# Gated mix of two attentions: three shared PSUM banks, raises in place, query tiles through DRAM, adding DMAs, and 372 blocks on VectorE

## The chip, the cores and the metric

The kernel runs on one core of a Trainium2 chip. The metric is the device time of one execution in microseconds (us); the time before is the median of three runs.

## The reference, cut to what matters

Two attentions over the same input are mixed by a gate of each row. S = 2048 rows, D = 512 columns, H = 32 heads of Dh = 16; everything is bfloat16.

```python
x = A_x
g = sigmoid((x * gate_w).sum(-1, keepdims=True))
# A: full attention, every row against every row
qkv = split(x @ A_wqkv)                                # q, k, v: H heads of 16
p = softmax(einsum("bhqd,bhkd->bhqk", q, k) * Dh ** -0.5)
a = einsum("bhqk,bhkd->bhqd", p, v) -> rows @ A_wo
# B: eight rows behind each row, two apart (row, row-2, ... row-14)
idx = pos[:, None] - 2 * arange(8)[None, :]; mask = idx >= 0
logits = einsum("bhsd,bhswd->bhsw", q, k[idx]) * Dh ** -0.5, -1e9 where masked
b = einsum("bhsw,bhswd->bhsd", softmax(logits), v[idx]) -> rows @ B_wo
out = g * a + (1 - g) * b
```

## The kernel before

**Attention A.** The 2048 queries are cut into four chunks of 512, and the heads into eight groups of four. A chunk and a group make a *period*; there are 32, in order of chunks. In a period the scores are computed transposed, in *blocks* of 128 keys by 512 queries: 16 key tiles by 4 heads, 64 blocks a period and 2048 in all. A head uses a strip of 32 rows of TensorE's array (16 for the keys, 16 for a bound that keeps the exponential in range, for which the queries' other 16 rows hold absolute values), so that blocks of different heads can run side by side. The key rows of all heads lie in `kt_all`, the values with a column of ones in `vp_all`.

**Two ways through the exponential.** Most blocks go to ScalarE: three or two blocks make a *set* (`qk`, into the PSUM rings rA and rB of three and two banks), one instruction takes the exponential of the set (`ex`, pT<-ring), and TensorE multiplies the result with the values into the sums of the period (`pv_run`, PSUM bank `acc`). The others go to VectorE (`d_set`, numbers a period in `n_dve`, 339 in all, always from the last three key tiles). A single score product fills the PSUM bank `D`; VectorE turns it into a 16-bit integer by one multiplication and addition (`p1`, dt_a<-D or wkv<-D: the second half of the buffers is the memory of the key and value weights, from period 8 on), which read as a bfloat16 is a rough power of two. Four *variants* of it, the integer raised by 0, 32, 64 and 96, are each multiplied with values that carry a weight of their own (`vd_all`, `NV` = 4), and their sum smooths the error. Three blocks make a group (`NGR`), so that one raise serves three blocks (`sh`, pd_a<-dt_a or pd_a<-wkv). Before, three raises of a group read the converted integers and write into one of three buffers `pd_a` each. Source and target are cut differently, six runs of 256 values into three runs of 512.

**End of a period.** `po1` transposes the sums out of PSUM (accT<-acc), the denominators are inverted (`po2`) and multiplied in (GpSimd, ott<-accT), `po3` transposes back, and after eight periods the output projection of the chunk follows (`ab_part`, `ab_ev`), which also adds in attention B.

**Queries.** `q_proj` makes the query tile of a period: 16 products of 32 columns from a copy of the weights in which each head's columns stand twice (`wq2`), a cast (qt<-misc_ps) and a mask that removes signs from half of the rows (qt<-qt,qmask).

**Attention B.** `b_tile` works on 128 rows at a time, 16 tiles. Keys and values are projected, written to DRAM (kv_scr) by SP's queue and gathered back shifted, four shifts at a time (ksh, vsh, three buffers `gat`). The arithmetic is GpSimd's, mostly on 256 columns an instruction: products with the queries (prod<-ksh,qb), additions that halve the row (prod<-prod, lg<-prod), a softmax together with VectorE and ScalarE (lg, mx, rr), products of values and weights (prod<-vsh,lg) and their additions (`av_add`: prod<-prod, ob<-ob,prod, ob<-prod, obb<-ob,prod; 14 a tile). At the end TensorE transposes obb into `obt`.

**Order of the work.** Nothing is issued as it comes: every step is an `Op` with an engine, a cost, a due time, predecessors and tokens of the buffers that it takes (`tok`, `Res`). `list_schedule` lays them out with a model of the chip, and the program is written in that order; `chain_on` fixes it on each engine. The model knows that some VectorE instructions and GpSimd's instructions exclude each other (`SB`, `GP`, the variable `port`). Idle time of TensorE is filled with products of zeros (`zeros`). All engines run in order, so an instruction that waits holds up everything behind it on its engine; this goes for SP's queue of DMAs too.

**PSUM.** Eight banks: five for the rings, one `acc`, one `D`, one `misc` for everything else (`misc_ps`).

Of the kernel before, what the change touches and what calls it, by code (L numbers as in the profile page):

```python
# [19 lines left out]
    n_dve=(3, 3, 6, 6, 6, 9, 9, 9) + (12,) * 24,  # L20
    dve_tiles=3,
# [15 lines left out]
DEXP = 56  # L37
NV = 4
NGR = 3
NPD = 3  # L40
# [5 lines left out]
NDL = 4  # L46
SPREAD = (0.75, 0.8)
STEP = 32.0
WEIGHTS = (0.240234375, 0.2021484375, 0.169921875, 0.142578125)
# [10 lines left out]

class Tok:
    def __init__(self, res):
        self.res, self.ops = res, []


class Op:

    def __init__(self, eng, occ, fn, dl, deps=(), alloc=(), use=(), lat=None, rel=0.0, name="",
                 mode="f", js=(), full=0.0, fill=False, scores=None, after=(), ride=False, parts=None):
        self.scores, self.ride, self.parts = scores, ride, parts  # L70
# [17 lines left out]
GFIRST = -300.0  # L88
PRE = 0.14
GP = lambda kind, n: [(False, PRE), (True, NS[kind] * n)]  # L90
# [11 lines left out]
P1D, SHD, LASTD, PO1D = -100.0, 2.0, 200.0, 300.0  # L102
# [56 lines left out]
def list_schedule(ops, zeros):  # L159
# [15 lines left out]

    def avail(o):
        t = o.ready
        for tk in o.alloc:
            r = tk.res
            n = len(r.order)  # L180
            if n >= r.cap:
                for u in r.order[n - r.cap].ops:
                    if u.done is None:
                        return INF
                    t = max(t, u.end + SELF[u.eng] if u.eng == o.eng else u.done)
        return t

    arr = Array()

    def start(e, o):  # L190
        t = avail(o)
        if t == INF:
            return t, 0.0
        if e != "pe":
            return max(free[e], t), o.dl
        t0, end, _, _ = arr.plan(o, t)
        rides = o.mode == "r" and arr.mode == "r" and end < arr.end + 0.05
        return t0, o.dl + ((ALONE if o.ride else KEEP) if o.mode != arr.mode else 0.0) - (RIDE if rides else 0.0)
# [3 lines left out]
    while len(out) < len(ops):  # L202
# [24 lines left out]
        if e == "pe":  # L227
            tz, n = arr.idle(o, t)
            if n > 0:
                z = zeros(n)  # L230
                tz = max([tz, avail(z)] + [u.t for tk in z.alloc[0].res.order[-2:] for u in tk.ops if u.done is not None and u.t < t])
                if tz + n * PASS + (0.0 if o.mode == "c" else SWITCH) <= t + 0.05:
                    for tk in z.alloc:
                        tk.res.order.append(tk)
# [3 lines left out]
        for tk in o.alloc:  # L238
            tk.res.order.append(tk)
# [16 lines left out]
        out.append(o)  # L256
        for s_ in succ.get(o, ()):
            left[s_] -= 1
            if left[s_] == 0:
                s_.ready = max([s_.rel] + [d.end + SELF[d.eng] if d.eng == s_.eng else d.done for d in s_.deps] + [d.t for d in s_.after])  # L260
                cand[s_.eng].append(s_)
# [4 lines left out]
def kernel(  # L266
# [29 lines left out]

    def misc_ps(shape, dtype=FP32, tag="misc"):
        return ps.tile(shape, dtype, tag=tag, bufs=1, name="misc_ps")
# [50 lines left out]
    def op(eng, occ, fn, dl, **kw):  # L349
        if any(tk.res is res.get("misc") for tk in kw.get("use", ())):  # L350
            dl -= URG[eng]
# [65 lines left out]
    wq2 = const.tile([128, DC, H, 2, DH], BF16, name="wq2")  # L417
# [6 lines left out]
    NH = NG // 2  # L424
    woarr = const.tile([128, NH, D], BF16, name="woarr")
    ident = const.tile([128, 128], BF16, name="ident")
    identf = const.tile([128, 128], FP32, name="identf")
    rowc = const.tile([128, 3], FP32, name="rowc")
    wts = const.tile([128, NV], BF16, name="wts")
# [7 lines left out]
    vd_all = const.tile([128, NV, NTD, H, DH + 1], BF16, name="vd_all")  # L437
# [4 lines left out]
    dt_a = const.tile([128, NDE * NGR * QW], BF16, name="dt_a")  # L442
    pd_a = const.tile([128, NPD * NGR * ROW], BF16, name="pd_a")
    wkv_l = wkv[:].rearrange("p c n -> p (c n)")
    dt_bufs = [dt_a[:, k_ * NGR * QW:(k_ + 1) * NGR * QW] for k_ in range(NDE)]
    dt_bufs += [wkv_l[:, k_ * NGR * QW:(k_ + 1) * NGR * QW] for k_ in range(NDL - NDE)]
    pd_bufs = [pd_a[:, k_ * NGR * ROW:(k_ + 1) * NGR * ROW].rearrange("p (q n) -> p q n", q=NGR) for k_ in range(NPD)]
    stage = [pd_a[:, k_ * DC * D:(k_ + 1) * DC * D].rearrange("p (c n) -> p c n", c=DC) for k_ in range(2)]
    ott2 = const.tile([128, 2, BPC, 32], BF16, name="ott2")
# [3 lines left out]
    e1 = const.tile([128, NT], FP32, name="e1")  # L453
    d1 = const.tile([128, NT], FP32, name="d1")

    def init_dve():
# [9 lines left out]
        for m in range(NV):  # L466
            V.memset(wts[:, m:m + 1], WEIGHTS[m] * 2.0 ** -DEXP)

# [10 lines left out]
    def init_pool2():  # L479
        make_identity(nc, identf[:])  # L480
# [19 lines left out]
    def load_x(sc):  # L500
        def s():
            xl = work.tile([128, W // 2, D], BF16, name="xld", tag="gat", bufs=NGA) if sc < NGA else stage[1]
# [4 lines left out]
    wst = {}  # L507

    def load_w(part):
        def s():  # L510
            if part == 0:
                wst["q"] = stage[0]
                out = wst["q"]
            else:
                out = wkv[:, :, (part - 1) * D:part * D]
# [17 lines left out]

    tw = tok("pd", NPD)
    xtok = [tok("gat", NGA) if sc < NGA else tok("pd", NPD) for sc in range(NC)]
# [6 lines left out]
    o_wq = op("sp", 0.5, load_w(0), -8.5, lat=12.5, alloc=[tw])  # L542
# [13 lines left out]
    def q2(E, i):  # L556
        def s():
            a0 = wst["q"][:, :, 4 * i * DH:4 * (i + 1) * DH]
# [6 lines left out]
    o_q2 = [op("dve", 0.5, q2(V, 0), 0.0, deps=[o_wq], use=[tw])]  # L565
    o_q2 += [op("pool", 1.5, q2(G, i), 4.0 + i, deps=[o_wq, o_k3[1]], use=[tw]) for i in range(1, NG)]
# [5 lines left out]
    o_warm = op("pe", 4.0, warm, -9.0, deps=[o_init_d], alloc=[tok("misc", 1)])  # L572
# [34 lines left out]
    def k_proj(i, sc, tag, dl, rel=0.0):  # L607
        st = {}
        tk = tok(tag, 1)
# [16 lines left out]
    def k_bound(i, dl):  # L626
        st = {}
        tk = tok("acc" if i == 0 else "misc", 1)
# [28 lines left out]
    for i in range(NG):  # L657
        o_kc[i] = []
        for sc in range(NC):
            if i == 0:  # L660
                o_kc[i].append(k_proj(i, sc, ("misc", "acc", "D", "misc")[sc], -2.0 + sc))
# [7 lines left out]
    def v_proj(h0, h1, tb, TB, tag, dl, rel=0.0):  # L669
        n = (h1 - h0) * DH  # L670
        st = {}
        tk = tok(tag, 1)
# [18 lines left out]
        def evd():  # L691
# [3 lines left out]
                            in0=_ap(vp_all[:, t0, h0, 0:1], [list(vp_all[:].ap[0]), [0, NV], [H * (DH + 1), nt], [1, n_]]),  # L695
                            in1=_ap(w, [list(w.ap[0]), [1, NV], [0, nt], [0, n_]]), op=ALU.mult)
# [7 lines left out]
        if nt > 0:  # L704
            d = op("dve", 0.0, evd, dl + 2.0, deps=[c], parts=TT(NV * nt * (h1 - h0) * (DH + 1)))
# [15 lines left out]
    def q_proj(pi, tag, dl, rel=0.0):  # L721
        c_, i = periods[pi]
        st = {}
        tk = tok(tag, 1)
        tq = tok("qt", 3)
        q_tok[pi] = tq

        def part(c0, c1):
            def s():
                if c0 == 0:  # L730
                    st["p1"] = misc_ps([128, QW], tag=tag)
                    qt_tiles[pi] = work.tile([128, QW], BF16, name="qt", tag="qt", bufs=3)
# [17 lines left out]
    for pi in range(1, NP):  # L750
        q_proj(pi, "misc", S0[pi] - 10.0, rel=S0[pi - 1] - 6.0 if pi > 1 else Q1REL)
# [3 lines left out]
    tzp, tzr = tok("misc", 1), tok("misc", 1)  # L755
# [10 lines left out]
    def zsig():  # L766
        A.activation(out=e1[:], in_=st_g["zp"][:, 0:NT], func=ACT.Exp, scale=-1.0)

    def zgate():
        V.tensor_scalar_add(out=d1[:], in0=e1[:], scalar1=1.0)  # L770
        V.reciprocal(out=g_sp[:], in_=d1[:])
        V.tensor_tensor(out=omg[:], in0=e1[:], in1=g_sp[:], op=ALU.mult)

    def zrows():
        st_g["zr"] = misc_ps([128, NT, TPC])
        for s_ in range(TPC):
            for j in range(4):
                mm(st_g["zr"][32 * j:32 * j + 32, :, s_], identf[:, 32 * s_:32 * s_ + 32], g_sp[:], True, True,
# [16 lines left out]
    WH = W // 2  # L795
# [3 lines left out]
    def b_tile(t):  # L799
# [26 lines left out]
        tk = tok("misc", 1)  # L826
# [3 lines left out]
        tk = tok("misc", 1)  # L830
# [539 lines left out]
```

## Time and profile before

| | us |
|---|---|
| median of 3 runs (825.62 to 826.81) | 826.49 |
| the profiled execution, its own time | 826.04 |
| its span, first to last instruction | 824.3 |
| ScalarE busy | 785.9 |
| TensorE busy (ends modelled) | 777.9 |
| GpSimd busy | 720.4 |
| VectorE busy | 706.3 |

The page names engines PE (TensorE), PEld (its weight loads), DVE (VectorE), ACT (ScalarE), POOL (GpSimd) and SP (the queue that issues DMAs). A group's row gives line, engine, operation, what is written and read, shapes and count; then busy time in us, the mean of one in ns, the idle time ahead of its instructions, and what ended most of it. As many instructions are recorded by a helper, most have the same line (L323, L332) and are told apart by the names of their tiles. Neighbouring instructions of an engine overlap by some hundredths of a microsecond, so busy time is less than count times mean. Issuing a DMA isn't counted as busy.

### The profile page before, as it was taken

To read this page: it belongs to the slowest core of one execution; us is meant where nothing else is said; L and a number is where in the kernel's file an instruction comes from. 1 tells how busy PE (TensorE), PEld (TensorE's weight loads), DVE (VectorE), ACT (ScalarE), POOL (GpSimd) and SP (SyncE) were. 2 spreads that over 40 slices of the span, in tenths; PEclk is the share of its full clock that TensorE was granted. 3 is DMA by queue.
4 is the path that set the end of the run, shared out by engine and by line. 5 is a ranking of instruction groups with operands and counts; after the bars stand their busy time and mean duration, and the time that the engine had idled before them with its cause. 6 is when DMAs were issued, how large, how long until landed. Compare 5 with 4: busy or idle time off the path is not lost.

```text
span 824.3 us, 18657 instructions
## 1 busy us (share of the span) xinstructions
PE 777.9 (94%) x7314; PEld 247.4 (30%) x7358; DVE 706.3 (86%) x1111; ACT 785.9 (95%) x706; POOL 720.4 (87%) x1196
## 2 busy tenths in 40 slices
PE   7999999999999999999999999999999999999996
PEld 4333433333322222222222222222222222222231
DVE  5456876788978999989999899999989899998987
ACT  3899999999899899999999999999999999999995
POOL 5097999999999999899999999899999999899960
PEclk9899999999999999999999999999999999999999
DMA  9203020112111220211112111211111211110000
GB/s 296 78 3 116 2 90 28 65 52 65 57 48 65 65 66 28 63 53 47 63 35 77 57 50 51 65 53 49 43 52 54 82 34 65 52 52 27 27 1 26
DMA packets 44440, 47.37 MB, mean 57 GB/s; under 512 B 2352, under 2 KB 41776, under 8 KB 44352
## 3 DMA queue, kind: packets, MB, share of 16 engines
q1 hardware_dynamic: 44352, 46.18, 17.6%
q8 instruction: 57, 0.93, 0.5%
q14 instruction: 31, 0.25, 0.1%
HBM read 39.85 MB, written 6.32 MB: 56 GB/s over the span
## 4 chain that ended last, share of the span: by engine, by line
ACT 47%; PE 31%; issue 18%; DVE 2%; DMA 1%; SPq 0%; DVEq 0%; ACTq 0%
ACT pT L323 46%; PE acc L332 11%; PE ring L332 9%; PE misc_ps L332 8%; PE D L332 3%; DMA xld<-in_A_x_dram 1%; ACT lg L323 1%; DVE pd_a L323 0%; DVE kt_all L323 0%; PE pxt L584 0%; PE misc_ps L1011 0%; DVE dt_a L323 0%; DVE qt L323 0%; DVE vp_all L323 0%; DVE wkv L323 0%
## 5 line engine op out<-in xcount | busy, mean ns | idle before, releaser
L323 ACT ACTIVATE pT<-ring 128x1536 bf16<-128x1536 f32 (+1 forms) x684 | 778.8, 1319 | 20.5 <-PE acc L332 14.0
L332 PE MATMUL ring<-qt,kt_all 32*128 32x512 bf16 x1709 | 272.0, 382 | 28.4 <-ACT pT L323 19.2
L323 POOL TENSOR_TENSOR prod<-prod 128x256 f32<-128x256 f32 x352 | 235.6, 677 | 13.2
L332 PE MATMUL acc<-pT,vp_all 128*17 128x512 bf16 (+1 forms) x1709 | 189.0, 385 | 0.3 <-DVE accT L323 0.2
L323 POOL TENSOR_TENSOR prod<-ksh,qb 128x256 f32<-128x256 bf16 x256 | 166.5, 673 | 22.5 <-DMA ksh<-kv_scr 21.7
L323 DVE TENSOR_SCALAR pd_a<-dt_a 128x1536 uint16<-128x1536 uint16 x195 | 180.4, 941 | 1.2
L332 PEld LDWEIGHTS <-kt_all 32*128 32x128 bf16 x2048 | 91.2, 91 | 294.1 <-issue 285.2
L323 DVE TENSOR_SCALAR dt_a<-D 128x512 uint16<-128x512 f32 x195 | 132.7, 680 | 39.2 <-PE D L332 38.5
L323 POOL TENSOR_TENSOR prod<-vsh,lg 128x256 f32<-128x256 bf16 x256 | 162.0, 652 | 0.0
L323 DVE TENSOR_SCALAR pd_a<-wkv 128x1536 uint16<-128x1536 uint16 x144 | 131.0, 945 | 1.9 <-PE acc L332 0.3
L332 PE MATMUL acc<-pd_a,vd_all 128*17 128x512 bf16 x1017 | 130.0, 381 | 0.0
L332 PE MATMUL D<-qt,kt_all 32*128 32x512 bf16 x339 | 128.7, 380 | 1.0 <-DVE kt_all L323 0.4
L323 DVE TENSOR_SCALAR wkv<-D 128x512 uint16<-128x512 f32 x144 | 98.2, 682 | 7.5 <-PE D L332 5.9
L332 PE MATMUL misc_ps<-z 128*32 128x512 bf16 x260 | 85.3, 387 | 1.6 <-DVE z L323 1.6
L332 PEld LDWEIGHTS <-vp_all 128*17 128x17 bf16 (+1 forms) x1709 | 43.7, 88 | 74.9 <-issue 66.6
L332 PEld LDWEIGHTS <-vd_all 128*17 128x17 bf16 x1356 | 42.3, 88 | 64.3 <-issue 51.5
L332 PE MATMUL misc_ps<-bw,xT 128*128 128x512 bf16 x162 | 51.6, 393 | 2.4 <-DVE kt_all L323 0.8
L323 POOL TENSOR_TENSOR ob<-ob,prod 128x256 f32<-128x256 f32 x64 | 45.5, 729 | 0.0
L332 PEld LDWEIGHTS <-z 128*32 128x32 bf16 x341 | 29.9, 96 | 42.2 <-issue 26.1
L332 PEld LDWEIGHTS <-xT 128*128 128x128 bf16 x576 | 30.2, 98 | 36.8 <-issue 31.8
L332 PE MATMUL misc_ps<-xT,wq 128*32 128x512 bf16 x512 | 40.5, 382 | 0.1
L323 DVE TENSOR_SCALAR_CACHE_REDUCE kt_all<-misc_ps,rowc 128x512 bf16<-128x512 f32 x32 | 23.8, 746 | 16.0 <-PE misc_ps L332 15.4
(85 smaller groups left out, 611.9 us busy)
## 6 DMA issues: line engine op xcount, KB each, us to landing
ksh<-kv_scr SPq DMA_DIRECT2D x32, 512.0 KB, 3.9
vsh<-kv_scr SPq DMA_DIRECT2D x32, 512.0 KB, 3.7
kv_scr<-kvs SPq DMA_DIRECT2D x16, 256.0 KB, 2.0
out_dram<-osb SPq DMA_DIRECT2D x16, 128.0 KB, 1.7
xld<-in_A_x_dram SPq DMA_DIRECT2D x3, 512.0 KB, 6.4
bw<-in_B_wqkv_dram SPq DMA_DIRECT2D x1, 1536.0 KB, 11.5
wkv<-in_A_wqkv_dram SPq DMA_DIRECT2D x2, 512.0 KB, 7.3
pd_a<-in_A_x_dram SPq DMA_DIRECT2D x1, 512.0 KB, 8.4
```

The costliest lines, as they stand in the source:

```text
L323: return chain_on(key, f(*a, **k))
L332: return chain(nc.tensor.matmul(out, lhsT=lhsT, rhs=rhs, start=start, stop=stop, **kw))
```

## The change

What it does:

- `tok` and `misc_ps`: the banks `acc`, `D` and `misc` become three banks (`Banks(3)`), of which the planner gives the one that is free first to whoever asks. Sums of a period keep theirs until they are transposed out, and at most two periods have one.
- `d_set`: a group has one buffer of two halves. The converted integers stay in the first; one copying raise by 64 fills the second (`sh`). Each half is multiplied with the values, then raised by 32 in place (`up`) and multiplied again. The first variant uses the plain values `vp_all`, so `vd_all` holds three weights instead of four, and four key tiles instead of three can be taken. Buffers: two, and three from period 8 on. The first conversion's score product now takes the buffer's token.
- `n_dve`: 372 blocks.
- `q_pair`: from the third period on, the queries of two periods (eight heads) are made by four products of 128 columns, cast, masked, written to DRAM (q_scr) by two DMAs and read back by two, in the layout of the heads' strips. All four are on SP's queue; the planner's due times put them 20 us ahead (`QD`). Query tiles have four buffers instead of three.
- Attention B: the weighted values of the first four shifts go to a buffer of their own (`av`), those of the others to `prod` (three buffers instead of two). In tiles 0 to 13, two DMAs issued by GpSimd add the second onto the first, a third one adds halves, and two GpSimd additions end it. In tiles 14 and 15 GpSimd adds everything, 14 additions each as before.
- Some small tiles share memory, some buffers are cut from two to one, and the planner's due times change.

The diff, cut to its core:

```diff
-    n_dve=(3, 3, 6, 6, 6, 9, 9, 9) + (12,) * 24,
-    dve_tiles=3,
+    n_dve=(3, 6, 6, 6, 9, 9, 9, 12) + (12,12,15) * 8,
+    dve_tiles=4,
...
-DEXP = 56
+DEXP = -2.0565
-NPD = 3
-NDL = 4
+NDL = 3
+ROWB = NGR * (QW + ROW)
-WEIGHTS = (0.240234375, 0.2021484375, 0.169921875, 0.142578125)
+WEIGHTS = (0.83984375, 0.70703125, 0.59375)
...
+class Banks(Res):
+    def __init__(self, n):
+        super().__init__(1)
+        self.banks = [[] for _ in range(n)]
...
     def misc_ps(shape, dtype=FP32, tag="misc"):
+        if tag in ("misc", "acc"):
+            bank, = [tk.bank for tk in now[0].alloc if isinstance(tk.res, Banks)]
+            tag = f"m{bank}"
         return ps.tile(shape, dtype, tag=tag, bufs=1, name="misc_ps")
...
     def tok(tag, cap):
-        if tag not in res:
-            res[tag] = Res(cap)
-        return Tok(res[tag])
+        name = "banks" if tag in ("misc", "acc") else tag
+        if name not in res:
+            res[name] = Banks(3) if name == "banks" else Res(cap)
+        return Tok(res[name], tag)
...
-    for pi in range(1, NP):
-        q_proj(pi, "misc", S0[pi] - 10.0, rel=S0[pi - 1] - 6.0 if pi > 1 else Q1REL)
+    q_proj(1, "misc", S0[1] - 10.0, rel=Q1REL)
+    def q_pair(pi, dl, rel):
...
+                    mm(st["p"][:], wq[:, c, 4 * i * DH:4 * (i + 2) * DH], xT[:, c, c_ * QW:(c_ + 1) * QW], c == 0, c == DC - 1)
...
+            V.tensor_copy(out=st["s"][:], in_=st["p"][:])
...
+            V.tensor_scalar(out=st["a"][:].bitcast(U32), in0=st["s"][:].bitcast(U32), scalar1=0x7FFF7FFF, scalar2=None,
+                            op0=ALU.bitwise_and)
...
+                SP.dma_start(out=_ap(q_scr[8 * pi + e:8 * pi + e + 1, :], [[2 * DH * QW, 8], [QW, DH], [1, QW]]),
+                             in_=src[:])
...
+                SP.dma_start(out=qt_tiles[pi + e][:], in_=_ap(q_scr[8 * (pi + e):8 * (pi + e) + 1, :], [[QW, 128], [1, QW]]))
...
+    for pi in range(2, NP, 2):
+        q_pair(pi, S0[pi] - QD, S0[pi - 2] - 2.0)
...
+        def av_sum(wp):
+            def s():
+                if wp is None:
+                    G.dma_start(out=av[:, 0:WP, :], in_=av[:, WP:WH, :], accum_op=ALU.add)
+                else:
+                    G.dma_start(out=av[:, wp:wp + WP, :], in_=st["av", wp][:], accum_op=ALU.add)
+            return s
...
+        def sums_of(wp, deps, use):
+            if t < NT - 2:
+                return op("pool", DMAQ, av_sum(wp), tb + 41, deps=deps, use=use, lat=DMAQ + DMAL, far=True, name=f"B{t}")
...
+                G.tensor_tensor(out=st["obb"][:, c0:c0 + HB], in0=av[:, 0, c0:c0 + HB], in1=av[:, 1, c0:c0 + HB], op=ALU.add)
...
-            pb = pd_bufs[d_count[1] % NPD]
-            a = op("dve", 0.0, sh(m, pb), tn + 1.5 + SHD * (m - 1) - ..., deps=deps, alloc=[tp], use=[g["td"]], ...)
-            b = op("pe", 0.0, pv(m, pb), tn + 4.5 + SHD * m, mode="c", js=g["js"], full=1,
-                   deps=[a, o_t0[pi]] + vs, use=[tp, acc_tok[pi]], name=f"dpv{pi}")
...
+        def sh():
+            i_ = d0.bitcast(U16)
+            V.tensor_scalar(out=pb.bitcast(U16)[:, :, 0:QW], in0=_ap(i_, [list(i_.ap[0]), [QW // 2, 2 * NGR], [1, QW // 2]]),
+                            scalar1=STEP * 2, scalar2=None, op0=ALU.add)
+        def up(m):
+            o_ = d0.bitcast(U16) if m == 1 else pb.bitcast(U16)[:, :, 0:QW]
+            return lambda: V.tensor_scalar(out=o_, in0=o_, scalar1=STEP, scalar2=None, op0=ALU.add)
...
+                    rhs = pb[:, n1, 0:QW] if m > 1 else d0[:, n1 * QW:(n1 + 1) * QW]
+                    pv_mm(pi, t_, j_, rhs, vd_all[:, m - 1, t_ - (NT - NTD)] if m else vp_all[:, t_])
...
+        b0 = dpv(0, list(g["p1"]), tn + 4.5)
+        b2 = dpv(2, [a], tn + 4.6)
+        c1 = op("dve", 0.0, up(1), tn + 5.0, deps=[b0, a], use=[g["td"]], parts=SB(NGR * QW), name=f"sh{pi}")
+        b1 = dpv(1, [c1], tn + 6.5)
+        c3 = op("dve", 0.0, up(3), tn + 5.5, deps=[b2, a], use=[g["td"]], parts=SB(NGR * QW), name=f"sh{pi}")
+        b3 = dpv(3, [c3], tn + 7.0)
```

In the program that comes out, 670 exponentials replace 683 of the sizes three and two (one of a single block stays in both), 124 copying raises and 248 in place replace 339 copying ones, GpSimd makes 56 additions of weighted values instead of 224 and issues 42 DMAs, SP issues 60 DMAs for query tiles, and the products of zeros go from 341 to 310.

More of the change, by code (lines that the diff above doesn't have):

```diff
@@ L174, in list_schedule, with freed @@
             cand[o.eng].append(o)
+    def freed(o, order, cap):
+        n = len(order)
+        t = 0.0
+        if n >= cap:
+            for u in order[n - cap].ops:
+                if u.done is None:
+                    return INF
+                t = max(t, u.end + SELF[u.eng] if u.eng == o.eng and not u.far else u.done)
+        return t
     def avail(o):
@@ L179, in avail, with take @@
             r = tk.res
[L180 to L185, printed above, removed]
-        return t
-    arr = Array()
+            t = max(t, min(freed(o, b, 1) for b in r.banks) if isinstance(r, Banks) else freed(o, r.order, r.cap))
+        return t
+    def take(o):
+        for tk in o.alloc:
+            r = tk.res
+            if isinstance(r, Banks):
+                tk.bank = min(range(len(r.banks)), key=lambda b: freed(o, r.banks[b], 1))
+                r.banks[tk.bank].append(tk)
+            r.order.append(tk)
+    arr, last = Array(), [0]
     def start(e, o):
@@ L237, in list_schedule @@
                     extra.append(z)
-        for tk in o.alloc:
-            tk.res.order.append(tk)
+        take(o)
         if e == "pe":
@@ L256, in list_schedule @@
         out.append(o)
+        if e == "act" and o.of is not None:
+            last[0] = o.of
         for s_ in succ.get(o, ()):
@@ new lines, in b_tile @@
+        tav = tok("av", 1)
+        b, sums = None, []
+        for hf, wp in halves:
+            tp_ = tok("prod", NPR) if hf else None
+            for n_, (w_, c0) in enumerate((w_, c0) for w_ in range(WP) for c0 in range(0, D, HB)):
+                al = ([tav] if hf == wp == 0 else [tp_] if hf else []) if n_ == 0 else []
+                us = [x for x in (tav, tp_) if x is not None and x not in al]
+                b = op("pool", 0.0, av_mul(hf, wp, w_, c0), tb + 40, deps=[lv[hf], a], after=[b], alloc=al, use=us + [tlg, tvs[hf]],
+                       name=f"B{t}", parts=GP("bf", HB))
+            if hf:
+                b = sums_of(wp, [b], [tav, tp_])
+                sums.append(b)
@@ L1338 @@
     for o in order:
+        now[0] = o
         o.fn()
```

327 lines of the change are left out of this document (179 added, 148 removed).

## The prediction

> **What bounds the kernel now.** I read, in this order, the page's engine rows and slices, the chain of waits, the groups, busy time by stage, the waits, and single instructions in order of time.
>
> ```profile
> PE 777.9 (94%) x7314; PEld 247.4 (30%) x7358; DVE 706.3 (86%) x1111; ACT 785.9 (95%) x706; POOL 720.4 (87%) x1196
> ...
> ACT  3899999999899899999999999999999999999995
> ...
> L323 ACT ACTIVATE pT<-ring 128x1536 bf16<-128x1536 f32 (+1 forms) x684 | 778.8, 1319 | 20.5 <-PE acc L332 14.0
> ```
>
> ScalarE's exponentials (pT<-ring) keep it busy from 19.7 us to 815.5 us. 684 of them cover 1709 blocks of 128 keys by 512 queries in 778.8 us of union time: 0.4557 us a block. Of the 20.5 us of idle time before them, 5.2 precede the first; some 15 lie between 19.7 and 815.5. After 815.5 a serial tail of 8.8 us ends the span of 824.3. So the time is start + ScalarE + tail, as long as the others keep up. How nearly they fail to, busy time by stage shows (columns: stretch, length, PE, PEld, DVE, ACT, POOL):
>
> ```profile
> 460.00:760.00 300.00, 289.64 (x2536) 83.78 (x2549) 277.34 (x408) 298.18 (x269) 280.04 (x468) 1.00 0.17 52
> ```
>
> All four are at 92 to 99%; a step that moves work between them has to be paid for by an engine with 7% left.
>
> **The change, part by part.** *ScalarE.* The blocks on VectorE go from 339 to 372, so ScalarE has 1676: 33 x 0.4557 = 15.0 us less. This is the whole gain of the forecast; everything below asks whether the cover holds.
>
> *VectorE.* Three blocks make a group: three conversions from PSUM (dt_a<-D) and three raises by a constant, which give the four variants. Before, each raise copies 1536 values into another buffer:
>
> ```profile
> L323 DVE TENSOR_SCALAR pd_a<-dt_a 128x1536 uint16<-128x1536 uint16 x195 | 180.4, 941 | 1.2
> L323 DVE TENSOR_SCALAR dt_a<-D 128x512 uint16<-128x512 f32 x195 | 132.7, 680 | 39.2 <-PE D L332 38.5
> L323 DVE TENSOR_SCALAR pd_a<-wkv 128x1536 uint16<-128x1536 uint16 x144 | 131.0, 945 | 1.9 <-PE acc L332 0.3
> ```
>
> (180.4 + 131.0) / 339 = 0.919 us each. After, 124 still copy and 248 work in place, a form that the trace lacks. Its nearest rows work in place with one source: the mask of a query tile (256 words, 1024 bytes) and the fill of a key row (2048 values, 4096 bytes).
>
> ```profile
> L323 DVE TENSOR_SCALAR qt<-qt,qmask x32: 253/514/881, 17.6 to 765.7; 128x256 uint32<-128x256 uint32 x32
> ```
>
> The columns 253/514/881 are shortest, median and longest in ns. The mean is 538 (the groups), so the mean wait is 538 - 253 = 285 ns, and the longest 628. The fill averages 1083; less the same wait, 798. A raise in place has 3072 bytes: between 253 and 798 in proportion, 616 ns, and with the mean wait 0.90 us. Bounds: 0.62 without a wait, 1.24 with the longest. I take 0.88 as pace, the overlap of neighbours off. So raising in place saves almost nothing on VectorE: 124 x 0.919 + 248 x 0.88 = 332 against 311 us, +21. The 33 more conversions cost 33 x 0.681 = +22. Query tiles made for eight heads at once need 17 casts and masks in place of 32: 15 x (0.684 + 0.538) = -18. Sum +25: 731 of some 809 us.
>
> In the steady part a period (four heads, 512 queries) took 52 x 0.4557 = 23.70 us, and VectorE worked 277.34 / 300 x 23.70 = 21.9 of it. After, with 13 blocks on average, it has +0.68 (a conversion), 4.33 x (0.919 + 2 x 0.88) - 12 x 0.919 = +0.58 and -0.61 (queries): 22.55 of 51 x 0.4557 = 23.24 us, 97%. It just fits.
>
> *GpSimd.* What does the wait do to the other side? GpSimd under the fill at 178.40:
>
> ```profile
> 178.40 0.89 DVE L323 TENSOR_SCALAR kt_all<-kt_all,rowc,negk 128x2048 bf16<-128x2048 bf16 x1
> ...
> 177.40 1.34 POOL L323 TENSOR_TENSOR prod<-ksh,qb 128x256 f32<-128x256 bf16 x2
> 178.70 0.84 POOL L323 TENSOR_TENSOR prod<-prod 128x128 f32<-128x128 f32 x1
> 179.62 0.31 POOL L323 TENSOR_TENSOR lg<-prod 128x64 f32<-128x64 f32 x1
> ```
>
> This addition takes 0.39 elsewhere: the fill waited for the product before it to end, and then held the addition for 0.45. Under the mask the same comparison gives 0.05. The copying raises show nothing of the kind. For 3072 bytes, in proportion, 0.32; 248 x 0.32 = +79 us (bounds 12 and 112).
> Against it, the additions of the weighted values go from 224 to 56 at (209.0 + 45.5 + 23.2 + 22.8) / 416 = 0.72: -121. In their place come 42 DMAs that add, issued by GpSimd. The page does not count DMA issues as busy; SP's four last ones took 2.13 us in all, 0.53 each, and the upper bound is a whole landing of a gather of the same 512 KB, 3.9. I take 1.0, nearer to SP's: +42. Sum -121 + 42 + 79 = 0.
> Is zero allowed? Its last instruction ended at 796.5; what hangs on it was folded by 802.4 and read only at 819.0. So it had 16.5 us to spare; with an end 15.0 earlier, 1.5 are left. It also idles 48 us between 39.3 and 797, of which the waits name 10.2 for the maxima; other work now stands in that place in the program, which gives some room.
>
> *The adding DMAs' landing.* GpSimd waits for two of them to land before it issues the third, and for the third before the last additions. In the new program order 3.8 to 6.9 us of other work (in one tile 1.9) stand in the first place and 5.7 to 7.2 in the second, the issue included, priced by the groups' rows. Nothing shows an adding DMA; 512 KB gathers land in 3.7 to 3.9, 128 KB in 1.7. Below the gather I exclude a gain, as the destination must be read too. If the bytes count twice, 1.0 + 2 x 2.9 = 6.8, with 2.9 = (3.9 - 1.7) x 512 / 384. I take 5, between them, where only the two short covers fail (some 4 us in all, inside that room); at 6.8 the shortfalls add up to 22.
> The Trainium skill, SBUF — State Buffer, section "SBUF: two separate sides", says of DMAs issued from GpSimd that "GPSIMD is locked out of the shared port pair" while VectorE runs a two-port operation and so can't write descriptors; it has a transfer of 620 ns take 3100. By that, an estimate from its figures, up to 2.5 us come on top of a landing, past the cover, and the forecast would be that of the GpSimd rival. No run here shows it yet; the 0.45 us above is the only such delay measured.
>
> *Queries through DRAM.* Four DMAs a pair of periods are put on SP's queue, where a gather waits for GpSimd's buffers (47 waits, longest 12.9 us). Cast 0.7, out 1.7, back 1.7 to 3.9, and one such wait: at most 19.2 of the 20 us of lead that the code asks for. Cover enough, so I cost it at nothing; were GpSimd late, the scores would wait with the gather, microsecond for microsecond.
>
> *TensorE.* By the groups: 480 narrow query products out (-38), 60 wide in (+19), 99 value products more (+13), 33 fewer behind ScalarE (-4), 33 score products moved to single ones (+7), 31 dummy products fewer (-10): -13 us. No new bound.
>
> *Banks.* With three shared banks two periods' sums may stand side by side, and a projection need not wait for one bank. That can take from ScalarE's waits "PE acc" 14.0 us at most, of which 3.1 belong to the start; I take nothing. A group now holds its buffer until the fourth variant is multiplied: three buffers hold 3 x 23.24 / 4.33 = 16.1 us, against some 10 that three conversions, three raises and the products take.
>
> *Sum.* The profiled execution took 826.04 with a span of 824.3, 1.7 around it; the median is 826.49. 826.04 - 15.0 = 811.0, and on the median 811.4.
>
> **Rivals.** *VectorE sets the pace (slower).* For it: 97%, in order, and raises in place now wait for a product as well; behind a waiting raise on VectorE stand conversions that free banks, behind those TensorE's in-order queue, and there the scores. Of its 1.8 us of idle time a period, mostly waits for D, none need vanish: 22.55 + 1.8 = 24.35 against 23.24, 1.1 longer in 24 periods, +26: 837. It decides from where VectorE's work and waits exceed 23.24, so with over 0.7 us of the waits left. Against: those waits come from slack.
> *GpSimd ends last (slower).* The landing of 6.8 (22 us), or a hold of 0.45 (+32), less the 1.5 spare: 832 to 842. It decides from 1.5 us on. Against: the room in its waits.
> *The banks give back waits as well.* 11 us of the 14.0, in part: 801 to 806.
> *Little is left.* Half of the 15 us goes into new waits of ScalarE: 816 to 825. That a raise in place isn't faster than a copy belongs here: it then holds GpSimd no longer than a copy does.
>
> **Chances.** Forecast 0.46 (806 to 816), banks 0.12, little left 0.08, VectorE 0.16, GpSimd 0.18. Below 824.8, that is faster by over 0.2% (about what a measurement of this kernel can tell from no change): 0.46 + 0.12 + 0.06 of little left = 0.64. Within 0.2%: the other 0.02 of it and 0.01 of GpSimd's. Above 828.1: the rest, 0.33. The range 803 to 838 leaves out half of the banks' case (0.06) and two thirds of GpSimd's (0.12).
>
> **What would show it.** Right: 670 exponentials at 0.456 us a block, idle below 20 us among them; in-place raises near 0.9; GpSimd's last instruction before 799. Wrong: VectorE over 97% with ScalarE waiting for products behind it; GpSimd waiting for an adding DMA, or SP for GpSimd with queries behind it.

## The result, and the profile after

The changed kernel takes 855.62 us (median of 4 runs, 854.26 to 856.9) against 826.06 (825.43 to 826.81) for the kernel before: the ratio is 1.0357, with a 95% interval from 1.0333 to 1.0381. It is 29.6 us slower, where 15 us less had been forecast. The profiled execution took 856.81, its span is 855.0.

The page of the changed kernel, engine rows, two of the rows in 40 slices, and the group of the exponentials:

```profile
PE 774.2 (91%) x6944; PEld 241.2 (28%) x7006; DVE 738.9 (86%) x1148; ACT 776.4 (91%) x693; POOL 679.2 (79%) x1058
...
ACT  2998989999899969989697999979999999999994
...
PEclk9999989999999979989797999989999999999999
...
L356 ACT ACTIVATE pT<-ring 128x1536 bf16<-128x1536 f32 (+1 forms) x671 | 768.8, 1294 | 56.0 <-PE ring L365 50.9
```

ScalarE's work did fall, from 778.8 us to 768.8. But its idle time ahead of the exponentials went from 20.5 to 56.0, and no engine is fuller than before: ScalarE 91% after 95%, TensorE 91% after 94%, GpSimd 79% after 87%, VectorE 86% in both. The kernel is not out of capacity; it waits. The loss is in bursts, too: most slices of ScalarE stay at 8 or 9, and a few drop to 6 and 7. TensorE's granted clock drops in slices nearby, and its mean over the kernel is 0.961, where it was 0.994. From start to end: the first exponential starts 1.1 us later, exponentials -10.0, idle time among them +36, the tail after the last one 12.2 instead of 8.8 (+3.4): +30.5, the spans' difference (+30.7) but for rounding.

Who waits for whom, in the waits of the changed kernel (columns: total us, times, longest us):

```profile
POOL rden L356 <- DVE rden L356: 64.0, 19, 10.1
ACT pT L356 <- PE ring L365: 50.9, 44, 5.1
PE misc_ps L365 <- DVE pd_a L356: 19.9, 27, 2.7
PE misc_ps L365 <- DVE wkv L356: 9.8, 10, 3.6
```

ScalarE waits for scores, TensorE for a raise of VectorE (pd_a, wkv), GpSimd for the inverted denominators that stand behind raises on VectorE. All of it leads to the raises. The tile view gives shortest, median and longest of them in ns, copying raises and those in place in one row:

```profile
L356 DVE TENSOR_SCALAR wkv<-wkv x102: 496/932/4678, 263.4 to 841.9; 128x1536 uint16<-128x1536 uint16 x102
L356 DVE TENSOR_SCALAR pd_a<-pd_a x270: 495/934/4516, 36.3 to 845.8; 128x1536 uint16<-128x1536 uint16 x135
```

Taken apart in the trace, the 124 copying raises take 0.89 to 0.96 us, and the 248 in place have a median of 0.81, below the 0.88 forecast. But the longest, 4.68 us, is almost four times the upper bound of 1.24 that the prediction set. Twelve raises, all of them in place, take over 1.3 us, 39.0 us together: 28 us more than 0.9 each. They stand in eight places. Eleven begin 0.5 to 2.6 us behind the start of a DMA av<-prod, which GpSimd issues, the twelfth 0.8 behind one av<-av. One in single instructions, in order of time (start, us, engine; merged neighbours are counted at the end, the wait ahead in brackets):

```profile
303.75 0.87 POOL L356 DMA_DIRECT2D av<-prod  x1 [0.30 <-POOL prod L356]
...
304.36 2.82 POOL L356 TENSOR_TENSOR prod<-ksh,qb 128x256 f32<-128x256 bf16 x4
304.40 4.68 DVE L356 TENSOR_SCALAR wkv<-wkv 128x1536 uint16<-128x1536 uint16 x1
...
306.87 2.52 POOL L356 TENSOR_TENSOR prod<-prod 128x256 f32<-128x256 f32 x3
...
308.60 0.80 POOL L356 TENSOR_TENSOR prod<-prod 128x256 f32<-128x256 f32 x1
...
309.13 0.60 PE L365 MATMUL misc_ps<-wkv,vd_all 128*17 128x512 bf16 x3 [3.62 <-DVE wkv L356]
...
311.45 1.45 ACT L356 ACTIVATE pT<-ring 128x1536 bf16<-128x1536 f32 x1 [4.33 <-PE ring L365]
```

GpSimd issues the DMA, then runs six instructions without standing; a raise that begins 0.04 us after the first of them ends only at 309.08. The seventh, at 308.60 (the last of the three above, shown again by itself), is the first for which GpSimd stands, 0.08 us, and the raise ends 0.48 us after the start of this instruction. Ten of the twelve long raises end like that, 0.13 to 0.48 us after the start of a GpSimd instruction ahead of which GpSimd stood 0.08 or 0.30 us.

A run of GpSimd instructions, with no stand of 0.06 us or more between them, doesn't do it by itself. In this trace 100 raises in place begin in a run that has no DMA at its head, with at least two more of its instructions to come: none takes over 1.22 us. In the runs behind a DMA 13 raises in place begin like that, and ten of them take over 2 us; 13 copying ones do, too, and none of these takes over 0.96.

TensorE, in order, stands 3.62 us behind the long raise; ScalarE has used up its rings by then and stands 4.33. The busy times by stage around it (columns as in the prediction: stretch, length, PE, PEld, DVE, ACT, POOL, the granted clock, DMA share, GB/s) show one more consequence:

```profile
304.00:309.00 5.00, 1.50 (x16) 0.41 (x16) 5.00 (x3) 2.37 (x2) 4.92 (x8) 0.85 0.81 113
309.00:315.00 6.00, 5.65 (x24) 1.07 (x24) 4.38 (x7) 2.48 (x2) 5.92 (x10) 0.50 0.78 193
315.00:321.00 6.00, 5.52 (x45) 1.54 (x44) 4.54 (x7) 4.23 (x4) 4.70 (x8) 0.77 0.00 0
...
307.50:317.60 10.10, 8.25 (x45) 1.72 (x48) 7.36 (x9) 3.93 (x3) 9.86 (x15) 0.50 0.60 123
...
123.20:129.90 6.70, 6.70 (x46) 2.47 (x49) 4.77 (x8) 4.00 (x4) 5.42 (x8) 0.50 0.45 86
```

TensorE is granted half the clock (0.50) from 307.5, still within its stand, to 317.6: in the 6 us after the stand it is busy 5.65 and gets 24 products done, against 45 in the stretch after, part of which has the full clock again. Six shorter stands, of 2.25 to 3.18 us, also have 0.50 within 2 us of their end; the last row is behind one of 2.34. The Trainium skill, TensorE: Matmul & The Clock Gate, Part 1, has the clock fall to half after an idle window of about 3.4 us. As a length of standing still this trace does not show it: six of the seven stands are shorter, and in the longest, of 3.62 us from 305.5, the clock was down after 2.0.

### The profile page after: what moved, and what is told of

Its sections match the earlier page's. It is cut to its first block, busy times and chain, and to the rows that moved or that the text cites. A ratio compares the mean times of both kernels' runs of the same rounds, so it can differ in the third digit from the quotient of the medians.

```text
span 855.0 us, 17993 instructions
## 1 busy us (share of the span) xinstructions
PE 774.2 (91%) x6944; PEld 241.2 (28%) x7006; DVE 738.9 (86%) x1148; ACT 776.4 (91%) x693; POOL 679.2 (79%) x1058
## 4 chain that ended last, share of the span: by engine, by line
PE 33%; ACT 27%; DVE 22%; issue 11%; POOL 4%; DMA 2%; DVEq 0%; ACTq 0%; POOLq 0%; SPq 0%
ACT pT L356 27%; PE misc_ps L365 23%; DVE pd_a L356 11%; PE ring L365 10%; DVE wkv L356 6%; POOL prod L356 3%; DMA ksh<-kv_scr 1%; DVE kt_all L356 1%; PE pxt L613 1%; DMA xld<-in_A_x_dram 1%; DVE kvs L356 1%; DVE qa L356 1%; DVE accT L356 0%; DMA kv_scr<-kvs 0%; DVE oat L356 0%
## 5 line engine op out<-in xcount | busy, mean ns | idle before, releaser
L356 ACT ACTIVATE pT<-ring 128x1536 bf16<-128x1536 f32 (+1 forms) x671 | 768.8, 1294 | 56.0 <-PE ring L365 50.9
L356 DVE TENSOR_SCALAR pd_a<-pd_a 128x1536 uint16<-128x1536 uint16 x270 | 246.4, 931 | 8.6 <-PE misc_ps L365 7.0
L365 PE MATMUL misc_ps<-pT,vp_all 128*17 128x512 bf16 (+1 forms) x1676 | 223.3, 394 | 0.7 <-DVE accT L356 0.2
L356 DVE TENSOR_SCALAR pd_a<-misc_ps 128x512 uint16<-128x512 f32 x270 | 177.8, 679 | 21.1 <-PE misc_ps L365 18.3
L356 POOL TENSOR_TENSOR prod<-prod 128x256 f32<-128x256 f32 (+1 forms) x256 | 183.7, 739 | 5.9
L365 PE MATMUL misc_ps<-qt,kt_all 32*128 32x512 bf16 x372 | 134.8, 391 | 4.3 <-DVE pd_a L356 2.2
L365 PE MATMUL misc_ps<-pd_a,vd_all 128*17 128x512 bf16 x810 | 110.0, 394 | 16.4 <-DVE pd_a L356 16.0
L356 DVE TENSOR_SCALAR wkv<-wkv 128x1536 uint16<-128x1536 uint16 x102 | 99.9, 987 | 1.2 <-PE misc_ps L365 0.6
L356 POOL TENSOR_TENSOR av<-vsh,lg 128x256 f32<-128x256 bf16 x128 | 85.5, 698 | 6.7 <-PE misc_ps L365 6.7
L356 POOL TENSOR_TENSOR prod<-vsh,lg 128x256 f32<-128x256 bf16 x128 | 86.5, 743 | 0.0
L356 DVE TENSOR_SCALAR wkv<-misc_ps 128x512 uint16<-128x512 f32 x102 | 67.9, 679 | 11.2 <-PE misc_ps L365 8.6
```

The lines of the kernel that those rows point to most:

```text
L356: return chain_on(key, f(*a, **k))
L365: return chain(nc.tensor.matmul(out, lhsT=lhsT, rhs=rhs, start=start, stop=stop, **kw))
```

## The experiments

The theory after this reading: *behind a DMA that GpSimd issues, VectorE's raises in place are shut out by GpSimd's following instructions until GpSimd waits for something; the long raises stop TensorE, and ScalarE with it.* Rivals: (1) the raises in place as such (their wait for a product, VectorE's order) and the many blocks; (2) the DMAs' own traffic or their landing; (3) the lower clock as a cause instead of a consequence. Each kernel is the changed one with the edit shown; the kernel before ran beside them at 825.6 to 825.9.

**A wait on GpSimd behind each DMA** (`e1_drain`). Two tiny instructions, of which the second needs the first, so that GpSimd waits once behind each of the 42 DMAs:

```diff
                 G.dma_start(..., accum_op=ALU.add)
+                G.memset(drn[:, 0:1], 0.0)
+                G.tensor_copy(out=drn[:, 1:2], in_=drn[:, 0:1])
```

> The changed kernel, with two one-column GpSimd instructions put behind each of its 42 adding DMAs, the second reading what the first wrote, so that GpSimd waits once; the order of everything else is kept. Theory (starved raises): behind a DMA that GpSimd issues, its next instructions follow each other so closely that an in-place raise on VectorE, which needs a gap between them, waits 2 to 4.5 us (12 raises, 28 us above 0.9 each in the changed kernel's trace), and the products, the banks and ScalarE wait behind it. Then no raise lasts over 1.4 us, ScalarE's idle time among the exponentials falls from 51 to some 20 us, the granted clock returns from 0.96 to 0.985 or more, and the time is 818 to 830 us. Rival 1 (in-place raises wait for products, VectorE is full at 97%): the gap changes nothing of that, 848 to 858. Rival 2 (the DMAs' traffic holds VectorE off): the long raises stay, 850 to 860.

Measured: 810.89 (809.48 to 812.26), ratio 0.9818 (0.98 to 0.9835), below the 818 to 830 expected of the theory and far from the 848 to 860 of rivals 1 and 2. The same place in the program in this kernel's trace, and its raises and exponentials:

```profile
295.50 0.87 POOL L356 DMA_DIRECT2D av<-prod  x1 [0.30 <-POOL prod L356]
296.08 0.40 POOL L356 MEMSET drn<- 128x1 f32 x1
296.54 0.18 POOL L356 COPY drn<-drn 128x1 f32<-128x1 f32 x1
...
298.20 0.95 DVE L356 TENSOR_SCALAR pd_a<-pd_a 128x1536 uint16<-128x1536 uint16 x1
```

```profile
L356 DVE TENSOR_SCALAR wkv<-wkv x102: 496/930/1217, 254.4 to 797.1; 128x1536 uint16<-128x1536 uint16 x102
L356 DVE TENSOR_SCALAR pd_a<-pd_a x270: 495/931/1218, 34.7 to 801.1; 128x1536 uint16<-128x1536 uint16 x135
...
L356 ACT ACTIVATE pT<-ring 128x1536 bf16<-128x1536 f32 (+1 forms) x671 | 764.8, 1322 | 17.3 <-PE ring L365 13.7
```

The longest raise is 1.22 us, inside the prediction's bound; the medians hardly change. 44.7 us are gone with some 27 us of *added* GpSimd work. The granted clock is 0.992, with the same work on TensorE: so the low clock goes with the long raises, as a consequence, and rival 3 falls. The steady part of the changed kernel and of this one:

```profile
260.00:760.00 500.00, 451.28 (x3708) 128.67 (x3743) 458.12 (x665) 463.07 (x413) 414.74 (x647) 0.95 0.37 94
```

```profile
260.00:760.00 500.00, 472.69 (x4047) 138.52 (x4043) 464.42 (x713) 493.49 (x444) 456.69 (x758) 0.99 0.38 97
```

In 500 us VectorE is busy about as long in both, but gets 713 instructions done in place of 665, and ScalarE's busy time goes from 463 to 493, at the same DMA share (0.37, 0.38) and with the same 42 adding DMAs: rival 2 loses its ground.

**The wait or the two instructions?** (`e9_no_wait`) The second instruction no longer needs the first:

```diff
-                G.tensor_copy(out=drn[:, 1:2], in_=drn[:, 0:1])
+                G.memset(drn[:, 1:2], 0.0)
```

> Two small GpSimd instructions behind each DMA as in the first experiment, but the second doesn't read the first, so GpSimd doesn't wait between them. If the wait is what lets the raises in, they starve again: 845 to 860 us, raises of over 2 us. If the added time alone (some 0.3 us a DMA) or any short instruction behind the DMA were enough, 808 to 820.

Measured: 850.39 (849.3 to 850.99), ratio 1.0298 (1.0283 to 1.0314), ten long raises. In its trace:

```profile
298.34 0.43 POOL L356 MEMSET drn<- 128x1 f32 x2
298.43 2.83 POOL L356 TENSOR_TENSOR prod<-ksh,qb 128x256 f32<-128x256 bf16 x4
...
298.41 4.74 DVE L356 TENSOR_SCALAR wkv<-wkv 128x1536 uint16<-128x1536 uint16 x1
```

As many instructions, a second memset for the copy and so one dependence fewer, and the raise takes 4.74 us again. It is the wait that lets VectorE in.

**Which DMAs** (`e5_drain_third`: the pair only behind the third DMA of a tile, av<-av, 14 of 42; `e10_drain_two`: only behind the first two, 28 of 42).

```diff
+                if wp is None:        # e10: if wp is not None
                     G.memset(drn[:, 0:1], 0.0)
                     G.tensor_copy(out=drn[:, 1:2], in_=drn[:, 0:1])
```

> The two small GpSimd instructions only behind the third adding DMA of each tile (av onto av), 14 of 42. In the changed kernel 11 of the 12 long raises came within a few microseconds of a DMA av<-prod and one, the shortest, behind av<-av. If each DMA starves only the raises right behind it, this mends little: 846 to 858 us, long raises stay. If one wait anywhere in the tile were enough to end a lasting state, 811 to 825.

> The two GpSimd instructions with the wait behind the first two adding DMAs of each tile only, 28 of 42; the counterpart of the run with the third alone. The starved raises stood nearly all behind these, so none over 2 us should be left and the time be that of the first experiment, 809 to 815. If the third DMA starves raises as well once the others don't, 818 to 835.

Measured: 850.39 (849.25 to 852.01) for the third DMA alone, with eleven long raises left; 815.32 (812.6 to 818.33) for the first two, with three left, of 2.56, 1.74 and 1.31 us, all behind av<-av, where none over 2 had been expected. So the first two DMAs of a tile make nearly all of the loss. In the changed kernel's trace GpSimd runs four to eight instructions without a stand behind 18 of the 28 DMAs av<-prod, and behind one of the 14 av<-av.

**The adding or the issuing?** In `e6_plain_dma` GpSimd issues the same 42 as plain copies; in `e2_sp_copy` SP does. Both leave out the additions, so what they compute is not the kernel's result.

```diff
-                G.dma_start(out=av[...], in_=..., accum_op=ALU.add)
+                G.dma_start(out=av[...], in_=...)        # e2: SP.dma_start
```

> The changed kernel with its 42 GpSimd DMAs as plain copies instead of adding ones (the additions are left out). If a DMA issue on GpSimd is what starves the raises, whatever the DMA does, the long raises stay and the time is 845 to 860. If the addition in the transfer is what matters, no raise lasts over 1.4 us and the time is 808 to 825.

> The changed kernel, with the 42 DMAs at the same places of the program but issued by SP, as plain copies of the same bytes (so the additions are left out). Starved raises: with no issue on GpSimd no raise lasts over 1.4 us, 815 to 830 us. Rival 2 (traffic): 42 DMAs of 512 KB still write the same buffers, so the long raises stay, and the time stays at 845 to 858. Rival 1 (products, VectorE full): unchanged, 848 to 858. SP's queue holds the copies where the products that they read end, which can cost some microseconds in all three.

By SP: 815.18 (812.97 to 816.65), ratio 0.9868 (0.9846 to 0.9889), no raise over 1.22 us. By GpSimd: median 833.84. Its seven executions scatter from 828.3 to 843.62; the ratio of the lower four is 1.0067 (1.0044 to 1.0089), and the profile is of one at 842.69. In this profile, where they land in 4.2 and 2.9 us, single instructions again:

```profile
298.56 0.59 POOL L356 DMA_DIRECT2D av<-prod  x1 [0.30 <-POOL prod L356]
...
298.74 5.61 DVE L356 TENSOR_SCALAR pd_a<-pd_a 128x1536 uint16<-128x1536 uint16 x2
```

Two raises in 5.61 us, with nothing added by a DMA: that GpSimd issues it is enough. Eight raises are long in this profile, which is of one of the three longest executions. It fits neither expectation in full: plain DMAs do it too, here fewer times. Whether the shorter executions have fewer long raises no trace shows.

**Copying raises in place of those in place** (`e3_copy_raise`; `e4_copy_raise_drain` with the pair of instructions as well). Three copying raises, in series, into the second half of the buffer:

```diff
-        c1 = op("dve", 0.0, up(1), ..., deps=[b0, a], parts=SB(NGR * QW), ...)
+        c1 = raise_(1, [b2], tn + 4.5)
-        c3 = op("dve", 0.0, up(3), ..., deps=[b2, a], parts=SB(NGR * QW), ...)
+        c3 = raise_(3, [b1], tn + 5.5)
```

> The changed kernel with every raise a copying one: the second half of the group's buffer is filled three times in turn from the integers (by 64, by 32, by 96), each after the product that read it. 372 copying raises of 0.94 us in place of 124 copying and 248 in place; the DMAs stay. Starved raises: the copying form is not held off by GpSimd, and doesn't hold it, so no raise lasts over 1.1 us; GpSimd's instructions get shorter by 248 x some 0.3 us in all; 812 to 830 us. Rival 1 (waits for products): three products in series instead of two in parallel make it worse: 855 to 880. Rival 2 (traffic holds VectorE): 850 to 870.

> Both: copying raises, and the two small GpSimd instructions behind each adding DMA. Starved raises: only the 15 masks of query tiles and a few fills can still be held off, so it differs from the kernel with copying raises alone by less than 6 us. Rivals 1 and 2: no difference beyond 6 us either, but from a base of 850 and above.

Measured: 932.1 (929.3 to 935.24) and 928.81 (924.9 to 930.8). No raise is over 0.96 us behind the same DMAs, so these copying raises are not shut out, as the 124 in the changed kernel are not; and the pair of instructions changes 3.3 us here where it changed 44.7 in the other form. This carries the theory. But that working in place is the condition does not follow. The mask of the new query tiles (qa<-qs) reads one buffer and writes another, both cut alike, where a copying raise cuts source and target differently. In the changed kernel one mask is shut out too, 1.3 us behind a DMA av<-prod; in e1 none is over 0.83:

```profile
L356 DVE TENSOR_SCALAR qa<-qs x15: 272/481/2221, 23.4 to 772.3; 128x256 uint32<-128x256 uint32 x15
...
658.45 2.22 DVE L356 TENSOR_SCALAR qa<-qs 128x256 uint32<-128x256 uint32 x1
```

Which difference between mask and copying raise counts, no run separates.

Also, the time of e3 misses what the theory expected, on the far side of rival 1: with one half as the target of all three, each raise waits for the products of the one before. In its waits:

```profile
DVE pd_a L356 <- PE misc_ps L365: 59.4, 90, 3.2
```

VectorE stands 59.4 us for products of TensorE, where it was 25.3 in the changed kernel. I read this as the price of another rotation of buffers, not of the copying form; how the rest of its loss comes about was not settled.

**What the other parts are worth, and how far the blocks go.** All with the pair of instructions: `e8_drain_339` with the old numbers of blocks, `e7_drain_384` and `e11_drain_396` with more.

```diff
-    n_dve=(3, 6, 6, 6, 9, 9, 9, 12) + (12,12,15) * 8,
+    n_dve=(3, 3, 6, 6, 6, 9, 9, 9) + (12,) * 24,          # e8: 339
+    n_dve=(3, 6, 6, 6, 9, 9, 9, 12) + (12,15) * 12,       # e7: 384
+    n_dve=(3, 6, 6, 6, 9, 9, 9, 12) + (12,15,15) * 8,     # e11: 396
```

> The first experiment's kernel with the blocks given to VectorE as before the change, 339 instead of 372. If the gain is ScalarE's 33 blocks alone, the time is that of the first experiment, 810.9, plus 33 x 0.456 = 15.0: 826, like the kernel before. If the other parts (three banks, raises in place, fewer query products) give something of their own, it is below 822; if they cost something that the blocks paid for, above 830.

> The first experiment's kernel (a wait behind every adding DMA) with 384 blocks on VectorE instead of 372. ScalarE has 12 x 0.456 = 5.5 us less; VectorE was busy 464 of 500 us in the steady part, 93%, and gets some 12 x (0.68 + 0.86) = 18 us over 24 periods, to 96%. If ScalarE still sets the pace: 805 to 808. If VectorE or TensorE's order is at its limit: 812 to 825.

> The same with 396 blocks: ScalarE 24 x 0.456 = 10.9 us less than with 372, VectorE at about 100% in the steady part by the same sum. If ScalarE set the pace: 800. By the sum VectorE does: 815 to 840.

Measured: 339 blocks 820.16 (819.46 to 821.35), 372 blocks 810.89, 384 blocks 842.25 (841.84 to 849.18), 396 blocks 878.18 (871.02 to 886.81). So everything but the blocks gives 825.6 - 820.2 = 5.4 us, and the 33 blocks 9.3, which is 0.28 a block. From the trace with 339 to that with 372 the exponentials take 15.6 us less; but the idle time among them grows by 3.9 (8.3 to 12.2) and the tail by 3.8 (8.5 to 12.3). Beyond 372 it turns. In the waits with 384 blocks:

```profile
POOL av L356 <- DMA av<-prod: 24.1, 10, 7.0
...
POOL obb L356 <- DMA av<-av: 7.7, 2, 4.2
```

GpSimd stands 31.8 us for the adding DMAs to land (with 372 blocks 2.1), and its last instruction ends at 829.3, long after the last exponential at 803.2. That is the prediction's rival "GpSimd ends last", though not at 372 blocks: in the planner's new order five of the 14 tiles have under 3 us of other work between the second DMA and the third, where with 372 two have. The pair's 27 us are in GpSimd's time in both, so what 384 would take without it is not shown. My own expectation for 384 missed it. With 396 blocks, above the 815 to 840 expected, GpSimd's last instruction ends at 861.4, and ScalarE stands 56.2 us for scores as well (longest 20.0); what holds those up was not followed.

The runs side by side; the excess is what the raises over 1.3 us take above 0.9 each, the time that of the median (e6: the profiled execution):

| kernel | long raises | excess, us | time, us | above e1, per us of excess |
|---|---|---|---|---|
| changed | 12 | 28 | 855.6 | 1.6 |
| e5, pair behind av<-av alone | 11 | 27 | 850.4 | 1.5 |
| e9, no dependence | 10 | 25 | 850.4 | 1.6 |
| e6, plain DMAs by GpSimd | 8 | 19 | 842.7 | 1.7 |
| e10, pair behind av<-prod alone | 3 | 2.9 | 815.3 | 1.5 |
| e2, plain DMAs by SP | 0 | 0 | 815.2 | |
| e1, pair behind each | 0 | 0 | 810.9 | |

Each microsecond of a shut-out raise goes with about 1.6 us of the kernel: the stand itself, and the time at half the clock, which is 66 us in the changed kernel's trace and 13 in e1's. How these two share it was not measured by itself, and e2, 4.3 us above e1 with no long raise, shows that the edits differ in more than this.

## Why the prediction was wrong, by its own steps

**The step that failed: the bounds of the raise in place.** "Bounds: 0.62 without a wait, 1.24 with the longest." The longest wait came from 32 masks, which in the trace of before wait for the one GpSimd instruction under way, at most 628 ns. That trace holds no DMA issued by GpSimd, so it could not show what such a DMA does to the next raise: a wait over up to six instructions. The pace was near, 0.88 forecast against a mean of 0.82 in e1; the bound was not, and twelve of 248 raises were enough. The two novelties were costed one by one, the DMAs on GpSimd's account and the raises on VectorE's; the cost lies in the pair. At the DMA I asked whom GpSimd waits for, and not who waits for GpSimd behind it.

**The place was named, the mechanism not.** The rival "VectorE sets the pace" had its chain: a waiting raise, TensorE in order behind it, the scores behind that; and its "wrong" sign, ScalarE waiting for products behind VectorE, is what the waits show. But it priced VectorE's waits for D, +26 by steady crowding, and 837 for it. The trace has VectorE at 86% and twelve long raises in eight places, seven of which stop TensorE for over 2 us and have it at half the clock, which no rival had. "GpSimd ends last" is not it either: in the changed kernel GpSimd's last instruction ends at 832.5, the last exponential at 842.9.

**The rule weighed.** From the Trainium skill, SBUF — State Buffer, section "SBUF: two separate sides", I took that GpSimd's descriptor writing is locked out by VectorE's two-port operations. Here the DMAs landed in a median of 5.6 (av<-prod) and 4.8 us (av<-av), near the 5 forecast, and GpSimd stood 3.8 us for them. Landings spread from 4.5 to 8.0, but long ones come without a raise in place beside the issue as well (6.83 us for the DMA at 260.35), so no run here shows a delay of that kind. What happened is the other direction, VectorE held up behind GpSimd's instructions. The Trainium skill, the same page, section "Who interferes with whom", says that whoever issues first has the shared ports for the whole instruction while the other blocks. By that, an estimate from this trace, a raise would wait for one instruction of GpSimd, some 0.65 us. The usual raise agrees, at most 1.22 us with 0.50 to 0.63 for the shortest; the 4.68 us behind a DMA is not in it.

**The rest of the sum stands,** when the shut-out is taken away (e1 against before): 810.9 against 811.0. Term by term it is less tidy:

- ScalarE: -15.0 forecast, its exponentials take 764.8 for 778.8, -14.0, at the forecast 0.456 us a block.
- The tail: left at 8.8 without a reason; it is 12.2 in the changed kernel and 12.3 in e1, where five raises and their products come behind the last exponential. Idle time among the exponentials gave 3.1 back (15.3 to 12.2 in e1).
- VectorE: +25 forecast, -0.8 measured (705.5 against 706.3 busy). The raises take 226.2 + 88.0 = 314.2 us, +3 where +21 stood, the conversions +15 for +22, the queries -18 as forecast.
- GpSimd: 0 forecast. Its last instruction came at 789.1 in e1, with the pair's 27 us in it, against 796.5 before and a limit of 799. The profile's page counts GpSimd's own DMA issues as busy, other than SP's. Without the pair (26.8) and these issues (25.5 + 12.2, a mean of 0.90 each, 1.0 forecast) its busy time is 691.9 - 64.5 = 627.4, 93 less than before. With 121 us of additions gone by the forecast's own price, an estimate is that the raises hold it for about 28 us, or 0.11 each. By that the 0.32 was too dear, inside its bounds.
- TensorE: -13 forecast, 760.3 against 777.9 in the trace, -17.6.
- Queries through DRAM: nothing, and no wait of TensorE for them is among the costly ones.
- Banks: nothing taken, up to 11 us as a rival. All other parts together give 5.4 at 339 blocks (e8), where the idle time among the exponentials is 8.3 for 15.3; the banks alone were not tried.
- A block moved was priced at ScalarE's whole 0.456 us. Taken singly it is worth 0.28 (e8 to e1), as part of it goes into the longer tail and into idle time. That e1 meets the 811 is luck: 5.4 us from the other parts, taken as nothing, and 5.7 too much for the blocks cancel.

## What to carry to other kernels

When a change adds two new things that touch the same resource from two engines, cost the pair, not only each: look for the longest stop that the one can give to the other. Engines that run in order pass one long stop on: 4.68 us of VectorE became 3.62 of TensorE and 4.33 of ScalarE here, with half the clock behind them. Where GpSimd issues a DMA and goes on without a wait while VectorE runs operations like these raises and masks, look at VectorE's longest instruction, not at its mean; two tiny dependent instructions behind the issue took 44.7 us off this kernel and made it 1.8% faster than the one before. And an order made by a planner has an edge: 12 more blocks than the best of the four numbers tried cost 31 us.

## What the runs showed of the hardware that I had not expected

- Behind a DMA issued by GpSimd, a raise in place on VectorE lasted up to 4.7 us, over up to six GpSimd instructions some 0.64 us apart, until GpSimd stood for something; with a dependent pair of small instructions behind the issue none was over 1.22 us. Runs as long without a DMA ahead of them held no raise over 1.22. It holds for adding DMAs and for plain ones, and for a mask from one buffer to another (2.22 us); copying raises that cut source and target differently (0.96 us at most) weren't touched. That it is the shared access of the two engines to memory is argued from which forms are hit, not shown; what the DMA changes in GpSimd stays open.
- Seven stands of TensorE of 2.25 to 3.62 us each had a granted clock of 0.50 within 2 us of their end; in the longest it fell 2.0 us after the stand began and stayed for 10 us. The mean over the kernel was 0.961 with twelve long raises and 0.992 without (e1), with the same work.
- An adding DMA of 512 KB within SBUF landed in a median of 5.6 and 4.8 us, a plain one of the same tiles in 4.2 and 2.9; its issue on GpSimd took 0.90 us in the mean, and some 0.6 for a plain one.
